# A fused attention and two-MLP kernel: the choice between two code paths moved to registers, the two paths' code swapped, the first loads made larger, and a new instruction order

## The chip, the cores and the metric

The kernel runs on one NeuronCore of a Trainium2 chip. The time is device microseconds of one launch: 628.85 us is the median of three runs (628.22 to 629.81). The engines are named as the profile names them: PE (TensorE, matmuls; PEld is its weight load), DVE (VectorE), ACT (ScalarE), POOL (GpSimd) and SP (SyncE, which here only issues transfers). Each has its own instruction stream and runs it in order; semaphores tie them together.

## The reference

The input is q, k, v for 2 batches, 8 heads, 768 positions and 64 dimensions, and three weight sets. Two scalars, `n_sink` = 4 and `window` = 128, say which keys a query sees.

```python
scores = scale * np.matmul(q, k.transpose(0, 1, 3, 2))
keep = is_sink | in_window               # key < n_sink, or 0 <= query - key < window
scores = np.where(keep, scores, -1000000000.0)
scores = scores - np.max(scores, axis=-1, keepdims=True)
a = np.exp(scores)
a = a / (np.sum(a, axis=-1, keepdims=True) + 1e-09)
attn = np.matmul(a, v)                   # heads joined: x is 1536 x 512
# first MLP
h = x @ w_in                             # 512 x 2048
g = np.where(h >= 1, h, np.where(h <= -1, 0.0, (h + 1) ** 2 / 4))
x = g @ w_out
# second MLP, d_ff = 1536
out = (1 / (1 + np.exp(-(x @ w_gate))) * (x @ w_val)) @ w_out2
```

## The kernel before, in words

The two scalars are inputs, so the program holds two paths. The banded path works where `n_sink` is at most 16 and `window` at most 129; it looks at 16 sink keys and two blocks of 128 keys per tile of 112 queries. The dense path takes any other values. The inputs of the runs take the banded path. Each engine's stream is: a common opening, a branch, the code of one path, the code of the other, and a common end.

The opening (`moe_chain_kernel`) loads the two scalars (`nw`), and q and k of the first two query tiles and v of the first, for the four head pairs, each pair in a transfer of its own, half of them issued by SP and half by ACT. POOL makes an identity matrix (`ident`), PE runs six matmuls on it, and POOL and DVE make the first mask. Then PE computes the scores of the first tile of all four pairs into two PSUM banks (L1242), DVE takes the row maxima of them (`row_tops`, L1186, eight times), and a flag, computed on POOL and DVE from the scalars and left in SBUF, is read by every engine into a register (L1246) and compared (L1247).

Before the diff the banded path's code stands right behind this branch, and the dense path's code behind it. So on the banded path the branch at L1247 goes straight on, and a jump at the end of the path leads over the dense path's code to the common end, where SP waits for the last transfers.

The banded path is not written in its final order. `Body.banded` and `Body.moe` record operations with reads, writes, a duration and a due time. `Plan.order` then places them by a list schedule: on each engine, the ready operation with the earliest due time comes first. A table of numbers at the top (`START`, `READY`, `FINISH`, `MOE_DUE`, `MOE_PACE`, `DRAIN`, `EARLY`, `LATE`, `SAME_MODE`, `BIAS`) sets when each engine is thought to begin and how early each kind is due. What comes out is fixed: nothing is chosen at run time. Where PE would stand idle in the plan's first 55 us, `Plan.fillers` puts matmuls of the identity on itself (L354), whose results nobody reads.

Per query tile and head pair PE does: scores (L927), transposes of the exponentials (L941), values (L968); per tile, four transposes that spread the inverse sums (L991). DVE takes row maxima (L1186) and the scaling (L982, L983, L1003), ACT the exponentials (L933) and most copies out of PSUM (L358). All of the second tile onwards is loaded by SP (L874).

Between these stand matmuls of the first MLP (L551 to L553, L596 to L598) on tokens that attention has finished. Its weights come as int64 words that hold float64 bits; SP loads them (`st`, L448), ACT or POOL rescales (L452, L454) and DVE does four more steps (L457, L460, L463, L466), then they are split in a high and a low part. After attention PE does the rest of the first MLP and the second one (L713, L799 to L801), and SP writes the result (L811) while the last matmuls run.

Of the kernel before, what the change touches and what calls it, by code (L numbers as in the profile page):

```python
# [51 lines left out]
DMA_LAT = 2.7  # L52
START = {"ACT": 0.9, "DVE": 2.1, "PE": 1.0, "SP": 1.1}
READY = {"tops": 0.2, "next": 0.5, "values": 1.5}

BIAS = {"DVE": 0.38, "POOL": 0.06, "ACT": -0.07}

SLOT_DUE = 2.55

FINISH = {"top": 3.59, "exp": 11.24, "turn": 13.87, "pts": 4.86, "values": -2.54, "div": 5.08, "out": -6.02}  # L60
MOE_DUE = 65.7
MOE_PACE = 5.86
DRAIN = 8.5
EARLY = 15.01
LATE = 62.91

ENTER, LEAVE = {"rows": 0.18, "cols": 0.14}, 0.09
SCORES_OF = 2
VALUES_OF = 4
SAME_MODE = 4.27  # L70
WARM = 6
# [70 lines left out]
class Plan:  # L142
# [40 lines left out]
    def order(self):  # L183
# [3 lines left out]
        free = {e: START.get(e, 0.0) for e in engines}  # L187
        held = {"DVE": 0.0, "POOL": 0.0}
        for o in self.ops:
            o.left = len(o.deps)  # L190
            for d in o.deps:
                d.next.append(o)
            if not o.left:
                for e in o.on:
                    ready[e].append((0.0, o))
        done, events, now, order, mode = 0, sorted({0.0, *START.values()}), 0.0, [], None
        running = []
# [105 lines left out]
class Body:  # L303
# [534 lines left out]


    def banded(self):  # L840

# [23 lines left out]
        def slot(k, due):  # L865
# [10 lines left out]
            mine, before = ("qk", p, at), ("qk", p, 1 - at)  # L876
            src = lambda j: self.a["qk"][b, j, p]
            if t < RAW:
                c0, first = pre["raw"][p]
                held = lambda j: cells("acc", 0, c0 + j * NQK, c0 + (j + 1) * NQK)  # L880
                own = lambda: pre["acc"][:, c0 + t * NQK:c0 + (t + 1) * NQK]
                rq = [k for j in (t - 1, t) if j >= 0 for k in held(j)]
            else:
                own, rq = (lambda: block(p, at)), [mine, before] if i else [mine]
            if t == 0:
                v, rv = (lambda: first), cells("acc", 0, c0 - P, c0)
                op("PRE", 0.0, 0.0, lambda: None, [], held(0), lat=0.0)
                op("PRE", 0.0, 0.0, lambda: None, [], held(1), lat=READY["next"] + 0.3 * p)
                op("PRE", 0.0, 0.0, lambda: None, [], rv, lat=READY["values"] + 0.2 * p)
# [14 lines left out]
            pt, pts = Buf(pt_r), Buf(pts_r)  # L904
            pr, mx = (Buf(pr_r), Buf(mx_r)) if t else (Kept(pre["rows"](p)), Kept(pre["mx"][:, 2 * p:2 * p + 2]))
            in_ring = [pr, mx] if t else []
            at_pr = [] if t else cells("acc", 0, pre["pr"][p], pre["pr"][p] + 2 * P)

            def keys(es):

                x = kept[p][es]
                if t < RAW:
                    a0 = c0 + (t - 1) * NQK + TQ
                    return pre["acc"][es, a0:a0 + 2 * (NQK + NS)].rearrange("p (c n) -> p c n", c=2)[:, :, :P]
# [119 lines left out]
    def dense(self):  # L1034

        nc, NP, S = self.nc, self.NP, self.S
        ident, lim = self.pre["ident"], limits(nc, self.pool(self.ctx, "lim"), self.pre["nf"])
        nk = S // P
# [56 lines left out]

FIRST_FLAG = 0x3F800000


def banded_test(nc, const, nf):

    ends, fits = const.tile([1, 8], F32, name="ends"), const.tile([1, 8], F32, name="fits")
    low, high, x = ends[:, :4], ends[:, 4:], nf[0:1].rearrange("p i w -> p (i w)")
    a, b = fits[:, :4], fits[:, 4:]
    v = nc.gpsimd
    for t, values in ((low, (0, 1)), (high, (NS, P + 1))):
        v.memset(t, 0.0)
        for i, y in enumerate(values):
            if y:
                v.memset(t[:, 2 * i:2 * i + 1], float(y))
    v.tensor_tensor(out=a, in0=x, in1=low, op=ALU.subtract)  # L1110
    v.tensor_tensor(out=b, in0=high, in1=x, op=ALU.subtract)
    return a, b


def banded_flag(nc, const, fits):


    a, b = fits
    flag = const.tile([1, 1], F32, name="flag")
    nc.vector.tensor_tensor_reduce(out=a, in0=a, in1=b, op0=ALU.mult, op1=ALU.max, scale=-1.0, scalar=0.25, accum_out=flag)  # L1120
    return flag.bitcast(I32)

# [67 lines left out]
def moe_chain_kernel(ctx: ExitStack, tc: tile.TileContext, a, out):  # L1190
# [9 lines left out]
        "acc": big.tile([P, KD * NT], F32, name="acc"),  # L1200
        "raw": [],
    }
    with tc.manual_schedule():

        nw, nf = const.tile([P, 4], I32, name="nw"), const.tile([P, 2, 2], F32, name="nf")
        nc.sync.dma_start(out=nw, in_=a["sizes"].bitcast(I32).rearrange("(o n) -> o n", o=1).to_broadcast([P, 4]))
        pre["nf"] = nf

        pairs = [(p, p * NT + S - TQ - 2 * NS, (nc.sync, nc.scalar)[p % 2]) for p in range(NP)]
        for p, c0, queue in pairs:  # L1210
            queue.dma_start(out=pre["acc"][:, c0:c0 + NQK], in_=a["qk"][0, 0, p])
        for p, c0, queue in pairs:
            queue.dma_start(out=pre["acc"][:, c0 + NQK:c0 + 2 * NQK], in_=a["qk"][0, 1, p])
        for p, c0, queue in pairs:
            v = pre["acc"][:, c0 - P:c0]
            queue.dma_start(out=v, in_=a["vb"][0, 0, p, :, 1])
            pre["raw"].append((c0, v.rearrange("p (c d) -> p c d", c=1)))
        nc.vector.tensor_copy(out=nf, in_=nw.rearrange("p (i w) -> p i w", i=2))
        pre["ident"] = const.tile([P, P], F32, name="ident")
# [7 lines left out]
        for i in range(WARM):  # L1227
            nc.tensor.matmul(out=pre["psum"][0][:, :P], lhsT=pre["ident"], rhs=pre["ident"], start=i == 0, stop=i == WARM - 1)
        pre["masks"] = masks = Masks(nc, const, nf, pre["acc"])
        fits = banded_test(nc, const, nf)  # L1230
        masks.make_first()
        flag = banded_flag(nc, const, fits)
        masks.weigh(masks.first)
        pre["mx"] = const.tile([TQ, 2 * NP], F32, name="mx0")
        pre["pr"] = [pairs[p // 2][1] + 3 * NQK + p % 2 * 2 * P for p in range(NP)]
        rows = lambda p: pre["acc"][:TQ, pre["pr"][p]:pre["pr"][p] + 2 * P].rearrange("p (e n) -> p e n", e=2)
        pre["rows"] = rows
        first = [pre["psum"][6 + e][:TQ].rearrange("p (i n) -> p i n", i=NP) for e in range(2)]
        for p, c0, _ in pairs:
            for e in range(2):  # L1240
                x = pre["acc"][64 * e:64 * e + 64, c0:c0 + NQK]
                nc.tensor.matmul(out=first[e][:, p], lhsT=x[:, :TQ], rhs=x[:, TQ + NS:], start=True, stop=True)  # L1242
        for p in range(NP):
            for e in range(2):
                row_tops(nc, rows(p)[:, e], first[e][:, p], masks.first, pre["mx"][:, 2 * p + e:2 * p + e + 1])
        on = nc.values_load(flag[0:1, 0:1], min_val=0, max_val=0x7F800000)  # L1246
    with tc.If(on < FIRST_FLAG) as branch:  # L1247
        with tc.manual_schedule(), ExitStack() as arm:
            body = Body(arm, tc, a, out, pre)
            body.banded()  # L1250
            body.moe(1)
            body.plan.run(body.banks, body.fill)
    with branch.Else():
        with tc.manual_schedule(), ExitStack() as arm:
            body = Body(arm, tc, a, out, pre)
            body.dense()
            body.moe(0)
            body.plan.run()


def layouts(inputs):
# [11 lines left out]
    vp = np.pad(vN, ((0, 0), (0, 0), (P, P), (0, 0)))  # L1273
    qk = np.zeros((B, len(tiles), NP, P, NQK), q.dtype)
    vb = np.zeros((B, len(tiles), NP, P, 2, P), v.dtype)
    for i, (q0, n) in enumerate(tiles):
        new = np.concatenate([kT[..., :NS], kp[..., P + q0 - NS:P + q0 + TQ]], axis=-1)
        qk[:, i, :, :, :n] = qT[:, :, :, q0:q0 + n]
        qk[:, i, :, :, TQ:] = new
        vv = np.concatenate([vN[:, :, :NS], vp[:, :, q0:q0 + W2 - NS]], axis=2)  # L1280
# [9 lines left out]
    def bands(w):  # L1290
# [5 lines left out]
        "v": np.ascontiguousarray(vN.reshape(B, NP, S // P, P, 2 * D).transpose(0, 1, 3, 2, 4)),  # L1296
        "qk": qk,
        "vb": vb,
        "w1": chunks(inputs["moe_w_in"]),
# [25 lines left out]
```

## Time and profile before

| | |
|---|---|
| runs, median | 628.85 us |
| profiled execution, its own time | 628.65 us |
| its span, first to last instruction | 626.9 us |
| around the span | 1.75 us |
| PE busy | 617.7 us, 3532 instructions |
| DVE busy | 509.4 us |
| ACT busy | 322.1 us |
| POOL busy | 90.3 us |
| HBM read, written | 50.60 MB, 3.15 MB |

The span is one execution on the chip. "Busy" of PE counts pipelined matmuls, so it says that matmuls followed each other, not how full the array was. A timeline row gives the start, the length of the merged stretch, the engine, the line of the kernel and the operation, the operands as output<-input, and in brackets how long the engine stood idle before it and what ended that. SPq and PEldq are the sequencers of SP and PE, which issue transfers, read registers and branch; that time is not counted as busy.

### The profile page before, as it was taken

What the parts mean: (1) busy time and instruction counts of PE and PEld (TensorE: products, weight loads), DVE (VectorE), ACT (ScalarE), POOL (GpSimd) and SP (SyncE); (2) the same over time, 40 slices, a digit from 0 to 9 for tenths busy, and PEclk for the clock granted to TensorE, in tenths of its full rate; (3) what the DMA queues carried; (4) which work ended last, traced back from release to release, by engine and by line L of the source; (5) the groups of instructions that cost most, each with busy time, mean ns of one, the idle gap of its engine ahead of it and who ended that gap; (6) DMA issues with size and microseconds to landing.
All of it is one profiled execution on the core that took longest, in us unless ns stands there. A gap on an engine that the chain in (4) does not pass through costs nothing.

```text
span 626.9 us, 9877 instructions
## 1 busy us (share of the span) xinstructions
PE 617.7 (99%) x3532; PEld 540.1 (86%) x3532; DVE 509.4 (81%) x1103; ACT 322.1 (51%) x738; POOL 90.3 (14%) x114
## 2 busy tenths in 40 slices
PE   8999999999999999999999999999999999999996
PEld 6788888888888888888888999998998998998995
DVE  5899998999996984458968797698898898895373
ACT  6999997656532441234335576563452452541430
POOL 1103320301000330012014320011011111120000
PEclk9999999999999999999999999999999999999999
DMA  6876764151540310001300012221221222100004
GB/s 200 261 214 195 231 183 158 62 198 38 167 135 4 114 55 30 1 0 35 101 35 0 1 35 98 72 101 33 81 89 54 81 68 78 58 0 1 1 36 172
DMA packets 28571, 54.48 MB, mean 87 GB/s; under 512 B 3296, under 2 KB 18400, under 8 KB 28512
## 3 DMA queue, kind: packets, MB, share of 16 engines
q1 hardware_dynamic: 27648, 53.10, 26.0%
q8 instruction: 30, 0.49, 0.3%
q10 hardware_dynamic: 864, 0.66, 0.3%
q14 instruction: 29, 0.24, 0.1%
HBM read 50.60 MB, written 3.15 MB: 86 GB/s over the span
## 4 chain that ended last, share of the span: by engine, by line
PE 95%; DMA 2%; SPq 2%; DVE 0%; ACT 0%; issue 0%; POOL 0%; POOLq 0%
PE bank L713 28%; PE bank L596 7%; PE bank L551 7%; PE bank L552 7%; PE bank L597 7%; PE bank L598 7%; PE bank L553 7%; PE bank L800 5%; PE bank L801 5%; PE bank L799 5%; PE bank L968 3%; PE bank L941 3%; PE bank L927 2%; SPq L874 1%; DMA st<-in_w 1%; PE bank L991 1%
## 5 line engine op out<-in xcount | busy, mean ns | idle before, releaser
L713 PE MATMUL bank<-xh,early 128*128 128x384 f32 x384 | 107.3, 334 | 0.0
L713 PE MATMUL bank<-late,early 128*128 128x384 f32 x432 | 85.0, 335 | 0.0
L713 PEld LDWEIGHTS bank<-late,early 128*128 128x128 f32 x432 | 76.0, 188 | 0.9
L358 ACT ACTIVATE early<-w 128x512 fp32r<-128x512 f32 (+1 forms) x59 | 35.4, 601 | 78.4 <-PE bank L713 34.6
L713 PEld LDWEIGHTS bank<-xh,early 128*128 128x128 f32 x384 | 70.2, 188 | 0.2
L713 PE MATMUL bank<-xl,early 128*128 128x384 f32 x192 | 64.2, 334 | 0.0
L809 DVE TENSOR_TENSOR acc<-bank,acc 128x512 f32<-128x512 f32 (+1 forms) x61 | 40.6, 677 | 23.8 <-PE bank L801 23.7
L570 ACT ACTIVATE tmp<-tmp 128x512 f32<-128x512 f32 x48 | 30.2, 631 | 46.5 <-DVE tmp L567 46.3
L933 ACT ACTIVATE pr<-pr,mx 112x256 f32<-112x256 f32 (+2 forms) x104 | 50.9, 494 | 0.1
L452 ACT ACTIVATE w<-st 128x512 f32<-128x512 f32 x60 | 39.4, 668 | 21.7 <-DMA st<-in_w 8.2
L463 DVE SCALAR_TENSOR_TENSOR w<-st,w 128x512 int32<-128x512 int32 x68 | 48.1, 708 | 0.7
L466 DVE SCALAR_TENSOR_TENSOR w<-st,w 128x512 int32<-128x512 int32 x68 | 46.9, 690 | 0.7
L365 DVE TENSOR_TENSOR early<-w,early 128x512 fp32r<-128x512 f32 (+1 forms) x63 | 40.4, 643 | 4.4 <-ACT early L358 4.4
L567 DVE TENSOR_SCALAR tmp<-bank 128x512 f32<-128x512 f32 x48 | 32.6, 683 | 14.0 <-PE bank L553 13.7
L358 ACT ACTIVATE gs<-tmp 128x512 fp32r<-128x512 f32 (+1 forms) x51 | 31.7, 623 | 23.3 <-DVE tmp L573 22.4
L612 DVE TENSOR_TENSOR acc<-bank,acc 128x512 f32<-128x512 f32 x36 | 24.3, 688 | 22.3 <-PE bank L598 22.2
L365 DVE TENSOR_TENSOR gs<-tmp,gs 128x512 fp32r<-128x512 f32 (+1 forms) x51 | 36.7, 723 | 6.4 <-ACT gs L358 5.8
L551 PE MATMUL bank<-xh,early 128*128 128x512 f32 x96 | 38.1, 397 | 0.0
L1186 DVE CUSTOM_DVE_ANT_0 pr<-bank,mask 112x256 f32<-112x256 f32 (+2 forms) x104 | 37.6, 403 | 0.5 <-PE bank L927 0.3
L596 PE MATMUL bank<-gs,early 128*128 128x512 f32 x96 | 37.9, 395 | 0.0
L552 PE MATMUL bank<-xl,early 128*128 128x512 f32 x96 | 37.5, 390 | 0.0
L553 PE MATMUL bank<-xh,early 128*128 128x512 f32 x96 | 37.5, 390 | 0.0
(179 smaller groups left out, 1490.2 us busy)
## 6 DMA issues: line engine op xcount, KB each, us to landing
st<-in_w SPq DMA_DIRECT2D x32, 512.0 KB, 3.5
v<-in_vb SPq DMA_DIRECT2D x52, 128.0 KB, 3.0
qk<-in_qk SPq DMA_DIRECT2D x48, 128.0 KB, 3.2
st<-in_wg SPq DMA_DIRECT2D x12, 512.0 KB, 3.3
st<-in_wv SPq DMA_DIRECT2D x12, 512.0 KB, 3.2
st<-in_wo SPq DMA_DIRECT2D x12, 512.0 KB, 3.3
out<-acc SPq DMA_DIRECT2D x11, 256.0 KB, 2.2
acc<-in_qk SPq DMA_DIRECT2D x8, 128.0 KB, 3.3
```

The costliest lines, as they stand in the source:

```text
L358: self.nc.scalar.activation(out=out, in_=x, func=AF.Copy)
L365: (self.nc.vector if e == "DVE" else self.nc.gpsimd).tensor_tensor(out=out, in0=x, in1=y, op=ALU.subtract)
L463: nc.vector.scalar_tensor_tensor(out=t(), in0=high(), scalar=-0x80000000, in1=t(), op0=ALU.bitwise_and, op1=ALU.bitwise_or)
L466: nc.vector.scalar_tensor_tensor(out=t(), in0=low(), scalar=29, in1=t(), op0=ALU.logical_shift_right, op1=ALU.bitwise_or)
L551: mm(out=out, lhsT=wh[:, c], rhs=mh, start=k == 0, stop=False)
L552: mm(out=out, lhsT=wh[:, c], rhs=ml, start=False, stop=False)
L553: mm(out=out, lhsT=wl[:, c], rhs=mh, start=False, stop=k == KD - 1)
L596: mm(out=out, lhsT=wh[:, c], rhs=gh, start=f == fs[0], stop=False)
L597: mm(out=out, lhsT=wh[:, c], rhs=gl, start=False, stop=False)
L598: mm(out=out, lhsT=wl[:, c], rhs=gh, start=False, stop=f == fs[-1])
L713: nc.tensor.matmul(out=out, lhsT=w[:, c], rhs=m, start=start and i == n == 0, stop=i == 1 and n == 2, skip_group_check=True)
L933: nc.scalar.activation(out=pr.ap[:n, e, :ks * P], in_=pr.ap[:n, e, :ks * P], func=AF.Exp, bias=mx.ap[:n, e:e + 1], scale=-1.0, accum_out=s ...
```

## The change

Five things change.

- The flag and its computation go (`banded_test`, `banded_flag`). `out_of_bands` lets each engine read the four words of the two scalars out of DRAM into registers right at the start, and compare them there.
- The branch now asks for the dense path. The dense path's code stands first and the banded path's code last, right ahead of the common end.
- The cast of the scalars, the first mask, the first tile's scores and their row maxima move behind the branch, into the banded path (`sizes`, `first_tops`). The scores of the four pairs and two heads go to eight PSUM banks instead of two.
- The first loads are five transfers instead of twelve: q and k of two head pairs together (256 KB, the layout of `qk` is changed for it), and v of all four pairs in one (`v0`).
- The table of numbers is another one, so the banded path's order is another one. The places where the first tiles lie in `acc` move with the loads.

```diff
-START = {"ACT": 0.9, "DVE": 2.1, "PE": 1.0, "SP": 1.1}
+START = {"ACT": 0.3, "DVE": 1.9, "SP": -1.5}
...
-EARLY = 15.01
-LATE = 62.91
+EARLY = 42.414
+LATE = -12.112
...
+    def first_tops(self):
+        nc, masks, NP = self.nc, self.pre["masks"], self.NP
+        self.sizes()
+        masks.make_first()
+        masks.weigh(masks.first)
+        for p in range(NP):
+            for e in range(2):
+                x = self.acc[64 * e:64 * e + 64, self.pre["raw"][0] + p * NQK:][:, :NQK]
+                nc.tensor.matmul(out=self.psum[2 * p + e][:TQ, :P], lhsT=x[:, :TQ], rhs=x[:, TQ + NS:], start=True, stop=True)
+        for p in range(NP):
+            for e in range(2):
+                row_tops(nc, self.rows(p)[:, e], self.psum[2 * p + e][:TQ, :P], masks.first, self.pre["mx"][:, 2 * p + e:2 * p + e + 1])
...
+def out_of_bands(nc, sizes):
+    words = sizes.bitcast(I32).rearrange("(o n) -> o n", o=1)
+    _, (ns, ns_high, win, win_high) = nc.values_load_multi_w_load_instructions(words, min_val=-2 ** 31, max_val=2 ** 31 - 1)
+    return (ns < 0) | (ns > NS) | (ns_high < 0) | (ns_high > 0) | (win < 1) | (win > P + 1) | (win_high < 0) | (win_high > 0)
...
+        raw, first_v = pre["raw"], pre["acc"][:, 3 * NT + TOK:3 * NT + 2 * TOK]
+        for t in range(2):
+            for h, queue in enumerate((nc.sync, nc.scalar)):
+                c = raw[t] + h * 2 * NQK
+                queue.dma_start(out=pre["acc"][:, c:c + 2 * NQK], in_=a["qk"][0, t, h].rearrange("p i n -> p (i n)"))
+        nc.scalar.dma_start(out=first_v, in_=a["v0"])
+        far = out_of_bands(nc, a["sizes"])
...
-        on = nc.values_load(flag[0:1, 0:1], min_val=0, max_val=0x7F800000)
-    with tc.If(on < FIRST_FLAG) as branch:
-            body.banded()
-            body.moe(1)
-            body.plan.run(body.banks, body.fill)
-    with branch.Else():
+    with tc.If(far > 0) as branch:
             body.dense()
             body.moe(0)
             body.plan.run()
+    with branch.Else():
+            body.first_tops()
+            body.banded()
+            body.moe(1)
+            body.plan.run(body.banks, body.fill)
```

On PE the start of the stream shows the moved branch. Before, the first tile's scores (L1242) and the read of the flag stand ahead of it:

```order
L1321 UNCONDITIONAL_BRANCH
L1228 MATMUL bank_92<-ident 128x128 x6
L1242 MATMUL bank_98<-acc 112x128
L1242 MATMUL bank_99<-acc 112x128
...
L1246 TENSOR_LOAD flag
L1247 COMPARE_AND_BRANCH
L927 MATMUL bank_92<-acc 112x256
```

Now two register reads (a pointer, then the four words) stand ahead of the six identity matmuls, and fifteen register operations ahead of the branch:

```order
L1311 UNCONDITIONAL_BRANCH
L1124 TENSOR_LOAD in_sizes_ptr
L1124 TENSOR_LOAD in_sizes
L1231 MATMUL bank_132<-ident 128x128 x6
L1234 REGISTER_ALU x15
L1234 COMPARE_AND_BRANCH
```

The dense path's rows follow; its last is the jump below, and the banded path starts behind it, some 3000 rows further on:

```order
L1234 UNCONDITIONAL_BRANCH
L858 MATMUL bank_125<-acc 112x128
L858 MATMUL bank_126<-acc 112x128
...
L858 MATMUL bank_132<-acc 112x128
L951 MATMUL bank_125<-acc 112x256
L951 MATMUL bank_126<-acc 112x256
```

So the first scores (now L858, banks 125 to 132) and the second tile's (now L951) both stand behind a branch that is taken.

On DVE the place is the first step on a weight (`w`), the clamp that follows POOL's rescaling. Before, it stands behind twenty row maxima of 256 columns; these are the last rows ahead of it and the first behind it:

```order
L1186 ISA pr,mx<-bank_96,mask_114 112x256
L1186 ISA mx 112x1
L1186 ISA pr,mx<-bank_93,mask_114 112x256
L1186 ISA mx 112x1
L457 TENSOR_SCALAR w<-w 128x512
L1003 TENSOR_TENSOR on<-on,bank_98 128x448
L982 TENSOR_SCALAR sm<-sm 112x8
L983 RECIPROCAL sm<-sm 112x8
```

Now it stands behind twenty-two of them, and a finished tile's two halves (`xh`, `xl`) stand ahead of it as before:

```order
L362 CAST xh<-on 128x4x112
L1190 ISA pr,mx<-bank_130,mask_147 112x256
L1190 ISA mx 112x1
L367 TENSOR_TENSOR xl<-on,xh 128x4x112
L1190 ISA pr,mx<-bank_128,mask_147 112x256
L1190 ISA mx 112x1
L1190 ISA pr,mx<-bank_125,mask_147 112x256
L1190 ISA mx 112x1
L459 TENSOR_SCALAR w<-w 128x512
L1190 ISA pr,mx<-bank_128,mask_147 112x256
```

The clamp moved two row maxima later. Over the whole banded path PE's operations are the same in kind and number, but for the identity matmuls between them, of which there are nine before (L354) and seven now (L356). Ahead of the first matmul of the MLP stand 52 scores and 72 values before, and 64 and 88 now.

## Rows read from the trace of the kernel before

**Rows 1.** Busy time by stretch: start:end, length, then each engine; granted clock.

```profile
0.00:5.00 5.00, 2.93 (x12) 2.64 (x12) 0.53 (x4) 0.00 (x0) 2.30 (x16) 1.00 0.44 132
6.60:45.00 38.40, 36.70 (x384) 29.38 (x385) 35.03 (x164) 37.17 (x135) 3.29 (x5) 1.00 0.79 243
45.00:621.70 576.70, 576.68 (x3121) 507.14 (x3120) 472.77 (x934) 284.00 (x605) 84.70 (x93) 1.00 0.23 75
```

**Rows 2.** What PE waited for: us in total, times, longest.

```profile
PE bank L927 <- DMA qk<-in_qk: 0.5, 1, 0.5
PE bank L991 <- DVE ie L360: 0.5, 1, 0.5
PE bank L941 <- ACT acc L933: 0.4, 1, 0.4
PE bank L991 <- ACT pr L933: 0.2, 1, 0.2
```

**Rows 3.** Timeline of the opening: start us, us, engine, line, operation, idle before.

```profile
0.73 0.20 POOL masks.py:197 MEMSET ident<- 128x128 f32 x1 [0.29 <-POOLq L1315]
1.35 2.93 PE L1228 MATMUL bank<-ident 128*128 128x128 f32 x12 [1.35 <-POOL ident masks.py:199]
5.02 1.44 PE L1242 MATMUL bank<-acc 64*112 64x128 f32 x16 [0.73 <-DMA acc<-in_qk]
6.62 1.99 PE L927 MATMUL bank<-acc 64*112 64x256 f32 x16 [0.17 <-DMA acc<-in_qk]
7.27 1.76 SPq L874 DMA_DIRECT2D v<-in_vb  x4
10.84 1.16 PE L354 MATMUL bank<-ident 128*128 128x128 f32 x8
```

**Rows 4.** Register reads and register operations of the flag: engine, operation, ns min/median/max, start.

```profile
L1246 PEldq TENSOR_LOAD <-flag x1: 485/485/485, 5.8 to 5.8; - x1
L1246 SPq FUSED_REGOPS  x1: 186/186/186, 6.9 to 6.9; - x1
L1246 DVEq TENSOR_LOAD <-flag x1: 542/542/542, 7.0 to 7.0; - x1
L1246 SPq SEQ_ASSERT  x1: 28/28/28, 7.1 to 7.1; - x1
```

**Rows 5.** The opening's read of the two scalars as a transfer: KB, us to landing.

```profile
nw<-in_sizes SPq DMA_DIRECT2D x1, 2.0 KB, 3.5
```

**Rows 6.** Branch and jump by engine: ns min/median/max, first to last start.

```profile
L1247 PEldq COMPARE_BRANCH  x2: 92/1878/3665, 6.4 to 618.8; - x2
L1247 SPq COMPARE_BRANCH  x2: 46/48/49, 7.2 to 622.6; - x2
```

**Rows 7.** SP's first instructions behind the jump: same columns.

```profile
L1321 SPq EVENT_SEMAPHORE  x10: 17/28/28, 625.5 to 626.8; - x10
```

**Rows 8.** The last seven output transfers, from 615 us on: issue, then landing in us.

```profile
L811 SPq DMA_DIRECT2D out<-acc x7: 332/333/446, 615.6 to 622.2; - x7
...
DMA to landing us min/median/max: 2.0/2.3/3.6
```

**Rows 9.** Code fetches ("instruction") in the transfers from 622.6 to 625.9 us.

```profile
q14 instruction: 3, 0.02, 2.7%
q8 instruction: 1, 0.02, 2.7%
```

**Rows 10.** Timeline around the first weight: POOL, DVE, PE.

```profile
22.54 0.67 POOL L454 TENSOR_SCALAR w<-st 128x512 f32<-128x512 f32 x1 [17.68 <-DMA st<-in_w]
23.25 0.43 DVE L457 TENSOR_SCALAR w<-w 128x512 f32<-128x512 f32 x1 [2.27 <-POOL w L454]
24.08 1.12 PE L927 MATMUL bank<-qk 64*112 64x256 f32 x8 [0.53 <-DMA qk<-in_qk]
32.01 0.57 PE L991 MATMUL bank<-ident,ie 112*128 112x112 f32 x4 [0.23 <-ACT pr L933]
```

**Rows 11.** A row maximum before 21 us: ns min/median/max, first to last start.

```profile
L1186 DVE CUSTOM_DVE_ANT_0 pr<-bank,mask x20: 371/420/425, 9.7 to 20.6; 112x256 f32<-112x256 f32 x20
```

More of the change, by code (lines that the diff above doesn't have):

```diff
@@ L52 @@
 DMA_LAT = 2.7
-START = {"ACT": 0.9, "DVE": 2.1, "PE": 1.0, "SP": 1.1}
[L54 to L63, printed above, removed]
-EARLY = 15.01
-LATE = 62.91
+START = {"ACT": 0.3, "DVE": 1.9, "SP": -1.5}
+READY = {"tops": 0.35, "next": (0.3, 0.5), "values": 1.0}
+BIAS = {"DVE": 0.693, "POOL": 0.41, "ACT": 0.365}
+SLOT_DUE = 2.235
+FINISH = {"top": -1.623, "exp": 2.295, "turn": 17.535, "pts": -3.643, "values": -3.859, "div": -7.538, "out": -23.001}
+MOE_DUE = 66.798
+MOE_PACE = 7.359
+DRAIN = 16.75
+EARLY = 42.414
+LATE = -12.112
 ENTER, LEAVE = {"rows": 0.18, "cols": 0.14}, 0.09
@@ L69 @@
 VALUES_OF = 4
-SAME_MODE = 4.27
+SAME_MODE = 6.12
 WARM = 6
@@ L188, in order @@
         held = {"DVE": 0.0, "POOL": 0.0}
+        events = sorted({0.0, *START.values()})
+        early = events[0]
         for o in self.ops:
@@ L194, in order @@
                 for e in o.on:
-                    ready[e].append((0.0, o))
-        done, events, now, order, mode = 0, sorted({0.0, *START.values()}), 0.0, [], None
+                    ready[e].append((early, o))
+        done, now, order, mode = 0, early, [], None
         running = []
@@ L837, in moe, with sizes, rows @@
             self.gated(p)
+    def sizes(self):
+        self.nc.vector.tensor_copy(out=self.pre["nf"], in_=self.pre["nw"].rearrange("p (i w) -> p i w", i=2))
+    def rows(self, p):
+        c = self.pre["pr"][p]
+        return self.acc[:TQ, c:c + W2].rearrange("p (e n) -> p e n", e=2)
+    def first_tops(self):
[10 more added lines that the diff above has]
+                row_tops(nc, self.rows(p)[:, e], self.psum[2 * p + e][:TQ, :P], masks.first, self.pre["mx"][:, 2 * p + e:2 * p + e + 1])
     def banded(self):
@@ L1200, in moe_chain_kernel @@
         "acc": big.tile([P, KD * NT], F32, name="acc"),
-        "raw": [],
+        "raw": [t * NT + TOK for t in range(RAW)],
+        "pr": [c + i * W2 for c in (3 * NT + 2 * TOK, NT) for i in range(2)],
     }
@@ L1227, in moe_chain_kernel @@
         for i in range(WARM):
[L1228 to L1233, printed above, removed]
-        pre["mx"] = const.tile([TQ, 2 * NP], F32, name="mx0")
[L1235 to L1245, printed above, removed]
-        on = nc.values_load(flag[0:1, 0:1], min_val=0, max_val=0x7F800000)
-    with tc.If(on < FIRST_FLAG) as branch:
-        with tc.manual_schedule(), ExitStack() as arm:
-            body = Body(arm, tc, a, out, pre)
-            body.banded()
-            body.moe(1)
-            body.plan.run(body.banks, body.fill)
-    with branch.Else():
+            nc.tensor.matmul(out=pre["psum"][7][:, :P], lhsT=pre["ident"], rhs=pre["ident"], start=i == 0, stop=i == WARM - 1)
+        pre["masks"] = Masks(nc, const, nf, pre["acc"])
+        pre["mx"] = const.tile([TQ, 2 * NP], F32, name="mx0")
+    with tc.If(far > 0) as branch:
         with tc.manual_schedule(), ExitStack() as arm:
@@ L1258, in moe_chain_kernel @@
             body.plan.run()
+    with branch.Else():
+        with tc.manual_schedule(), ExitStack() as arm:
+            body = Body(arm, tc, a, out, pre)
+            body.first_tops()
+            body.banded()
+            body.moe(1)
+            body.plan.run(body.banks, body.fill)
 def layouts(inputs):
```

62 lines of the change are left out of this document (19 added, 43 removed).

## The prediction, on record before the changed kernel ran

> **What bounds the kernel now.** I read the busy time by stretch first [rows 1]. [...] In the first 5 us there are only the identity matmuls. [...] The work itself is the same; the order lists the same PE operations but for two identity matmuls. The waits of PE come next: four behind the branch, 1.6 us together [rows 2], and 0.17 at 6.62 [rows 3]; the last of them ends at 32.0 [rows 10]. Then the opening in order of time [rows 3], the branch and the end.
>
> The profiled execution took 628.65 us, its span and 1.75 us around it; the median of the runs is 628.85. I sum against 628.65 and compare with 628.85; differences under 0.3% (1.9 us) count as no change, being about what a measurement of this kernel can tell.
>
> **The opening.** Before, PE starts on the second tile's scores at 6.62 us [rows 3]; all that follows on PE hangs on that start. Now each engine must read registers, compare, take a branch and get code that does not lie next to it. The steps on PE:
>
> - Entry at 0.73 us, when POOL began before [rows 3].
> - Two register reads. Read out of SBUF one word took 0.49 us on PE and 0.54 on DVE [rows 4]. The trace has no read out of DRAM. Its bounds are that 0.5 from below and, far off, a whole transfer of the same words, 3.5 us [rows 5], from above, so 1.0 to 7.0 for the two. I take 1.0, since the row is the same instruction. POOL makes its two reads ahead of `ident`, so PE's identity matmuls begin 0.62 us (1.35 - 0.73) after 1.73, at 2.35, instead of 1.35.
> - Fifteen register operations. Rows near it are an assertion of 28 ns and a fused pair of 186 ns [rows 4], so 0.03 to 0.09 each, 0.4 to 1.4 together; I take 0.9: 3.25 us.
> - The branch and the code. Before, it goes straight on and costs 92 ns on PE at 6.4 us. The jump at the end of the path shows what going elsewhere costs: 3.67 us on PE, 2.9 on SP (622.6 to 625.5) [rows 6, 7]. 3.25 + 3.7 is 6.95 us. PE's eight first scores take 0.9 (sixteen passes of L1242; their 1.44 us holds a wait for the second loads).
>
> The second tile's scores then begin at 7.85 instead of 6.62: **+1.2 us**. The lower bound is where the loads bind again: the first q and k landed at 5.0, so 5.9, a gain of 0.7. With reads of 3.5 us each the upper bound is 13.9, a loss of 7.2. DVE goes the same way and has cast and mask to make while PE does the first scores; I cost that at nothing too, or up to 1 us if DVE comes no earlier than PE. SP issues three loads first and pays 2.9, so it enters within 0.5 us of its 7.27 before [rows 3]. The five larger loads hide behind the branch, as do the eight banks; I cost both at nothing. If the branch were free, the data would bind, and larger loads would then be worth the 0.17 that PE waited at 6.6 [rows 3].
>
> [...]
>
> **What PE loses up to 45 us.** DVE stood 2.27 us before its clamp of the first weight at 23.25, since POOL waited for its load until 22.54 [rows 10]. PE's waits of 0.5, 0.5 and 0.2 us lie behind it, at 24 to 32 us [rows 10], one of them on DVE's `ie` [rows 2]. In the new order the clamp stands two row maxima later, 0.42 us each [rows 11], and DVE itself is about 1.2 late while SP's load is 0.5 late. The stall shrinks to 2.3 - 0.8 - 1.2 + 0.5, about 0.8. PE has twelve more scores and sixteen more values ahead of its first MLP matmul, so it can bridge that. I count the three waits as gone, **-1.2 us**, bounds 0 (they come back elsewhere) and -1.8 (all of them). The wait for the first exponentials, 0.4, stays. Two identity matmuls fewer: eight passes took 1.16 us [rows 3], so a matmul of two passes is 0.23 to 0.29, and two are **-0.45**, provided their gaps are really closed; else 0. From 45 us on I cost the new order at nothing. PE has covered all of it there, and if a weight came late, each us of delay would show in full.
>
> **The end.** The last issue is at 622.2 us, and its landing took 3.6, to 625.8; the median of the seven last is 2.3, the lowest 2.0 [rows 8]. The same stretch has four fetches of code [rows 9], those of the jump, on the same transfer engines. SP itself is back only at 625.5 [rows 7]. Without the jump both go: 622.2 + 2.3 is 624.5, **-1.3 us**, bounds 0 (the late packet had another cause; SP's return then hides in it) and -1.6.
>
> **Sum.** 628.65 + 1.2 - 1.2 - 0.45 - 1.3 = 626.9 us, 1.95 under the median, just past the bound of 1.9.
>
> **The rivals.**
>
> - *A deeper gain.* The code comes while PE would wait for data anyway. Then the scores begin at 5.9 and the opening gives -0.7: 628.65 - 0.7 - 1.2 - 0.45 - 1.3 = 625.0. For it speaks that everything up to 5.0 us is idle for PE [rows 1]; against it, that the fetch cannot begin before the registers are known, and 3.67 us from 3.25 ends behind 5.0. Chance 0.22.
> - *The two ends cancel.* The reads out of DRAM are slower: the geometric mean of 0.49 and 3.5 [rows 4, 5], 1.3 us each, makes the opening +2.8 and the sum 628.5. That such a read goes further than one out of SBUF speaks for it. Chance 0.20. [...]
> - *Slower: PE enters late and at half rate.* PE's twelve passes on `ident` took 2.93 us, 0.23 each, where later ones took 0.12 to 0.14 [rows 3], while the granted clock reads 1.00 [rows 1]. Before, 0.73 us of rest stood between them and the scores. Now they end near 5.3 and PE rests until it has its code. If fetches of five engines in turn hold it until 9.5 (2.5 later than summed) and it has fallen back by then, first and second scores take 0.9 + 1.7 us more: 626.9 + 2.5 + 2.6 = 632.0. It decides from the point where opening and half rate together cost 4.85, past the 2.95 that the other terms give and the 1.9 of the bound. Against it: with a rest of 2 us or less nothing in this trace shows a fall. Chance 0.14. [...]
>
> That the change does not do what it says could be true of the banks alone: if DVE's mask comes later than the first scores, eight banks change nothing. The sum holds that already.
>
> **How the numbers follow.** The forecast, 626.9 with its own range 625.7 to 628.0, gets 0.44; the rivals 0.22, 0.20 and 0.14. Faster by over 0.3% (under 626.97) is half of the forecast's, 0.23, and the deeper gain, 0.22, and a little of the second: 0.47. Slower by over 0.3% is nearly all of the last, 0.13. Same is the rest, 0.40. The range leaves out about a tenth on each side: 624.4 to 629.8.
>
> **What would show it.** Right: DVE's and PE's branch near 3 us and the next instruction some 3 us later; the second tile's scores between 7.3 and 8.5 us; no PE wait over 0.3 us between 20 and 45 us; the last output transfer landing within 2.4 us, with SP already waiting for it. Wrong: scores before 6.6 us (the fetch hides), register reads over 1 us each, identity-like pitch of 0.23 us in the first scores, a wait of PE after 45 us, or a last landing as late as before.

## The result, and the profile after

The changed kernel takes 636.35 us, the median of 6 runs (634.83 to 636.52); beside it the kernel before took 629.44 (628.22 to 630.03). The ratio is 1.0106, with a 95% interval of 1.0091 to 1.0121. The forecast was 626.9, within 624.4 to 629.8: the change went the other way. The profiled execution took 636.37 us, with a span of 634.6.

The first view is the busy time by stretch of the kernel after (start:end, length, then PE, PEld, DVE, ACT, POOL, the granted clock, DMA share and GB/s). They answer to the stretches of [rows 1]: from the second tile's scores to 45 us, from there to the last matmul, and the end.

```profile
12.30:45.00 32.70, 30.33 (x310) 23.50 (x307) 29.21 (x132) 29.00 (x106) 3.14 (x4) 1.00 0.76 231
45.00:631.40 586.40, 584.18 (x3197) 512.53 (x3194) 485.19 (x941) 285.30 (x614) 121.36 (x124) 1.00 0.24 77
631.40:634.60 3.20, 0.03 (x1) 0.00 (x0) 0.42 (x1) 0.00 (x0) 0.00 (x0) 1.00 0.45 164
```

Against the spans of before these rows give the whole difference of 7.7 us:

| | before | after | difference |
|---|---|---|---|
| second tile's scores begin at | 6.6 | 12.3 | +5.7 |
| PE idle from there to 45 us | 38.40 - 36.70 = 1.70 | 32.70 - 30.33 = 2.37 | +0.7 |
| PE idle from 45 us to the last matmul | 0.02 | 586.40 - 584.18 = 2.22 | +2.2 |
| PE busy in both stretches | 613.38 | 614.51 | +1.1 |
| from the last matmul to the end | 626.9 - 621.7 = 5.2 | 3.2 | -2.0 |

PE's busy time is longer though it has two identity matmuls fewer: the thirty-two passes of scores on `acc` took 5.1 us, 4.2 before. The opening lost most. Here is its timeline, in the columns of [rows 3]:

```profile
4.71 0.20 POOL masks.py:197 MEMSET ident<- 128x128 f32 x1 [4.26 <-issue]
5.33 2.93 PE L1231 MATMUL bank<-ident 128*128 128x128 f32 x12 [5.33 <-POOL ident masks.py:199]
9.24 0.17 DVE L843 CAST nf<-nw 128x4 f32<-128x4 int32 x1 [9.24 <-issue]
10.51 2.05 PE L858 MATMUL bank<-acc 64*112 64x128 f32 x16 [2.24 <-issue]
10.95 2.94 SPq L897 DMA_DIRECT2D v<-in_vb  x4
12.32 1.09 PE L951 MATMUL bank<-acc 64*112 64x256 f32 x4
13.97 1.55 PE L951 MATMUL bank<-acc 64*112 64x256 f32 x12 [0.55 <-issue]
```

PE's scores of the second tile stand at 12.32 where they stood at 6.62, and after four passes they stop until 13.97: "issue" says that PE waits for nothing that the profile shows. That it waits for its next instructions is a reading: among the transfers a packet of code ("q8 instruction"), taken here for PE's, stands between 10.9 and 12.6 us, as another does at 7.9 behind the branch. SP enters the path at 10.95 instead of 7.27.

The register reads of the same stretch (engine, operation, ns min/median/max, start):

```profile
L1124 PEldq TENSOR_LOAD <-in_sizes_ptr x1: 946/946/946, 0.8 to 0.8; - x1
L1124 PEldq TENSOR_LOAD <-in_sizes x1: 2878/2878/2878, 1.8 to 1.8; - x1
L1124 SPq TENSOR_LOAD <-in_sizes_ptr x1: 2778/2778/2778, 2.1 to 2.1; - x1
L1124 SPq TENSOR_LOAD <-in_sizes x1: 888/888/888, 4.9 to 4.9; - x1
```

The reader is to see that it is not the kind of read that makes it slow: PE's first and SP's second take 0.9 us, and all that are under way between 2.2 and 4.6 us, the five engines' together, take 2.8 to 3.0. Then the register operations and the branch, in the same columns:

```profile
L1234 PEldq ALU_OP  x15: 37/43/43, 5.4 to 6.8; - x15
L1234 PEldq COMPARE_BRANCH  x1: 3349/3349/3349, 6.9 to 6.9; - x1
```

Fifteen operations take 1.5 us, 0.1 each from start to start, and the branch 3.35. What PE waits for behind 12.3 us (us in total, times, longest) answers to [rows 2]:

```profile
PE bank L951 <- DMA acc<-in_qk: 1.0, 1, 1.0
PE bank L951 <- DMA qk<-in_qk: 0.8, 2, 0.5
PE bank L715 <- DVE bank L362: 0.7, 1, 0.7
PE bank L951 <- issue: 0.6, 1, 0.6
PE bank L1015 <- POOL xh L364: 0.5, 1, 0.5
PE bank L1015 <- DVE mx L1190: 0.5, 1, 0.5
PE bank L965 <- DVE on L1027: 0.4, 1, 0.4
```

And the last outputs, against the 2.0/2.3/3.6 of [rows 8]:

```profile
DMA to landing us min/median/max: 1.7/2.0/2.0
```

### The profile page after: what moved, and what is told of

It reads as the page before. It is cut to its first block, busy times and chain, and to the rows that moved or that the text cites. A ratio compares the mean times of both kernels' runs of the same rounds, so it can differ in the third digit from the quotient of the medians.

```text
span 634.6 us, 9924 instructions
## 1 busy us (share of the span) xinstructions
PE 619.3 (98%) x3528; PEld 540.5 (85%) x3528; DVE 516.9 (81%) x1086; ACT 316.4 (50%) x723; POOL 126.2 (20%) x137
## 4 chain that ended last, share of the span: by engine, by line
PE 91%; DVE 5%; SPq 2%; DMA 1%; issue 1%; POOL 0%; ACT 0%; DVEq 0%
PE bank L715 27%; PE bank L598 7%; PE bank L599 7%; PE bank L600 7%; PE bank L553 6%; PE bank L554 6%; PE bank L555 6%; PE bank L803 5%; PE bank L802 5%; PE bank L801 5%; PE bank L951 3%; PE bank L992 3%; PE bank L965 3%; DMA qk<-in_qk 1%; PE bank L1015 1%
## 5 line engine op out<-in xcount | busy, mean ns | idle before, releaser
L360 ACT ACTIVATE early<-w 128x512 fp32r<-128x512 f32 (+1 forms) x46 | 26.3, 573 | 74.7 <-PE bank L803 28.1
L468 DVE SCALAR_TENSOR_TENSOR w<-st,w 128x512 int32<-128x512 int32 x68 | 51.7, 761 | 0.7
L465 DVE SCALAR_TENSOR_TENSOR w<-st,w 128x512 int32<-128x512 int32 x68 | 47.5, 698 | 0.6
L454 ACT ACTIVATE w<-st 128x512 f32<-128x512 f32 x61 | 40.3, 666 | 12.7 <-DMA st<-in_w 6.9
L367 DVE TENSOR_TENSOR early<-w,early 128x512 fp32r<-128x512 f32 (+1 forms) x53 | 37.1, 702 | 5.8 <-POOL early L364 5.4
L367 DVE TENSOR_TENSOR gs<-tmp,gs 128x512 fp32r<-128x512 f32 (+1 forms) x49 | 35.2, 719 | 4.6 <-ACT gs L360 4.0
L364 POOL TENSOR_SCALAR early<-w 128x512 fp32r<-128x512 f32 x19 | 13.7, 719 | 123.6 <-PE bank L715 58.2
```

Of the source, the lines that this page charges most:

```text
L360: self.nc.scalar.activation(out=out, in_=x, func=AF.Copy)
L367: (self.nc.vector if e == "DVE" else self.nc.gpsimd).tensor_tensor(out=out, in0=x, in1=y, op=ALU.subtract)
L465: nc.vector.scalar_tensor_tensor(out=t(), in0=high(), scalar=-0x80000000, in1=t(), op0=ALU.bitwise_and, op1=ALU.bitwise_or)
L468: nc.vector.scalar_tensor_tensor(out=t(), in0=low(), scalar=29, in1=t(), op0=ALU.logical_shift_right, op1=ALU.bitwise_or)
```

## The experiments

Fifteen kernels were run, each beside the kernel before on the same chip; ratios are to that. Four of them and the changed kernel form a ladder, in which each step adds one part of the change:

| step | median | ratio to before, 95% interval |
|---|---|---|
| large first loads | 629.78 | 1.0016 (1.0007 to 1.0024) |
| and register reads | 630.92 | 1.0020 (1.0012 to 1.0029) |
| and first scores behind the branch, eight banks | 630.32 | 1.0017 (1.0006 to 1.0028) |
| and the dense path's code first | 634.30 | 1.0082 (1.0065 to 1.0100) |
| and the new table: the changed kernel | 636.35 | 1.0106 (1.0091 to 1.0121) |

So two of the five parts carry the loss, 4.0 and 2.1 us; the other three cost 1 us together. By the ratios they are 4.1 and 1.5 us, and the intervals of the last two rows overlap, so the table's share is the less certain one.

### The code swap

The changed kernel with the banded path first again:

```diff
-    with tc.If(far > 0) as branch:      # dense, Else: banded
+    with tc.If(far < 1) as branch:      # banded, Else: dense
```

> The changed kernel with the banded path's code ahead of the dense path's again; all else as changed. Theory (code that a taken branch goes to must be fetched, 3.35 us on PE at 6.9 us, and once more between 12.8 and 14.0): PE's branch under 0.3 us, first scores near 7.9 instead of 10.5, no gap of over 0.5 us in the second tile's scores, SP in the path near 8.1 instead of 10.95; PE gains 3.7 to 5 us, the jump at the end costs 2 again: 633 to 635 us. Rival (the register reads out of DRAM are the cost, and the code would have to be fetched on a straight path too): the opening stays, the end adds 2: about 638 us.

Measured: 633.57 us, 1.0065 (1.0052 to 1.0078), 2.8 below the changed kernel. PE's branch there:

```profile
L1234 PEldq COMPARE_BRANCH  x2: 95/1898/3702, 6.8 to 624.2; - x2
```

95 ns at 6.8 us, and 3.7 us for the jump at 624.2. SP enters at 8.00, and the first scores and the second tile's follow each other without a gap:

```profile
8.08 2.05 PE L858 MATMUL bank<-acc 64*112 64x128 f32 x16
9.92 2.33 PE L951 MATMUL bank<-acc 64*112 64x256 f32 x16
```

The theory holds. The first scores are at half pitch here too (sixteen passes in 2.05 us, 1.13 in the next run), with no rest ahead of them.

Next, with the dense path's code left out altogether:

```diff
     with tc.If(far > 0) as branch:
-            body.dense() ...
+            pass
```

> The changed kernel with the dense path's code left out (the other arm is empty), so the taken branch goes a few instructions ahead. Theory (distance is what costs: the code behind is then at hand): PE's branch under 0.5 us, first scores near 7.9, PE gains 3.7 to 5 us, the end as in the changed kernel: 631 to 633 us. Rival (any taken branch throws away what was fetched ahead): branch 2 to 3.4 us as now, 636 us.

Measured: 631.60 us, 1.0034 (1.0021 to 1.0047). This is a taken branch too, but a short one:

```profile
L1234 PEldq COMPARE_BRANCH  x1: 232/232/232, 6.9 to 6.9; - x1
8.17 1.13 PE L858 MATMUL bank<-acc 64*112 64x128 f32 x16
```

What costs is the distance, not that the branch is taken: 0.23 us here, 3.35 over the dense path's code. This kernel has neither the late entry nor the jump at the end. The swap alone on the kernel before (`on < FIRST_FLAG` turned to `on >= FIRST_FLAG`, the two bodies exchanged):

> The kernel before with one edit: the dense path's code ahead of the banded path's. Flag in SBUF, scores ahead of the branch, loads and order as before. Theory (a taken branch to far code costs PE 3.35 us, and a second stall of 1 us follows): PE's branch near 6.4 us takes 3.3 to 3.7, second tile's scores at 9.9 instead of 6.62, SP in the path near 10.2 instead of 7.27; the end 2 us shorter: 631.5 to 633 us. Rival (the fetch lies beside row maxima and exponentials that are to be done anyway): scores before 8.5, 627.5 to 629 us.

Measured: 632.27 us, 1.0052 (1.0036 to 1.0067). PE's branch takes 3.75 us at 6.4, the second tile's scores begin at 10.30, 3.7 later, and run at half the pitch:

```profile
5.03 2.05 PE L1242 MATMUL bank<-acc 64*112 64x128 f32 x16 [0.76 <-DMA acc<-in_qk]
10.30 4.18 PE L927 MATMUL bank<-acc 64*112 64x256 f32 x16 [3.22 <-issue]
```

Sixteen passes of L927 took 1.99 us before [rows 3] and 4.18 here. So this kernel loses the rest itself and goes on at half pitch. That the second follows from the first is not shown: PE was at half pitch ahead of the branch already (the 2.05 us), and two kernels without a far branch, with the large loads alone and with the new table alone, took 3.62 and 3.55 us for the same sixteen passes (below). The last matmul ends 5.9 us later (627.6 for 621.7), which is 3.7 + 2.2, and the end is 1.9 shorter. The second stall that the theory named did not come.

### The register reads and the fetch

`out_of_bands` moved ahead of the loads on SP and ACT:

```diff
+        far = out_of_bands(nc, a["sizes"])
         nc.sync.dma_start(out=nw, ...)
         ...
-        far = out_of_bands(nc, a["sizes"])
```

> The changed kernel with the register reads ahead of the first loads on SP and ACT. Theory (the second read took 2.9 us since the first loads run at the same time; SP's and ACT's second reads, after them, took 0.9): every read 0.9 us, PE's and DVE's branch about 2 us earlier (near 4.9), loads issued 1.9 us later; the first scores then wait for the loads: 634.5 to 636.5 us. Rival (something other than the loads holds the reads until 4.6 us): reads still end near 4.6, loads land 3 to 4 us later: 637 to 640 us.

Measured: 635.18 us, 1.0094 (1.0080 to 1.0109). The reads took 0.96 and 0.53 us on PE:

```profile
L1124 PEldq TENSOR_LOAD <-in_sizes_ptr x1: 957/957/957, 0.8 to 0.8; - x1
L1124 PEldq TENSOR_LOAD <-in_sizes x1: 525/525/525, 1.8 to 1.8; - x1
```

The loads had slowed them, then: the same four words took 0.53 us here and 2.88 in the changed kernel. But the branch, now at 4.5 us, took the time back, and the first scores waited 5.1 us for no load, as the theory had it, but at "issue". Its two rows, here and with three of the five loads moved behind the branch, which leaves two fifths of the bytes ahead of it:

```profile
L1234 PEldq COMPARE_BRANCH  x1: 6289/6289/6289, 4.5 to 4.5; - x1
```

```diff
-        for t in range(2): (loads of tile t)
-        nc.scalar.dma_start(out=first_v, in_=a["v0"])
+        load(0)
...
+            load(1)                                   # in the banded path
+            nc.scalar.dma_start(out=first_v, in_=a["v0"])
             body.first_tops()
```

> The changed kernel with the register reads ahead of the loads on SP and ACT, as in the run of that name, and the loads of the second tile and of v moved behind the branch, so that a third of the bytes is in flight when the code is fetched. Theory (PE's code took 6.29 us there, and 3.35 in the changed kernel, since its fetch waits behind the loads): PE's branch 3.4 to 4.5 us from 4.5, first scores by 9.5, 632.5 to 634.5 us. Rival (something other than the loads holds the fetch): branch over 6 us, 635 to 637 us, since the second tile's loads now come later too.

```profile
L1234 PEldq COMPARE_BRANCH  x1: 4309/4309/4309, 4.5 to 4.5; - x1
```

4.31 us instead of 6.29 at the same start: the fetch waits behind the loads, as the theory has it. The transfers say the same: the packet taken for PE's code begins 3.9 us after the branch with all loads ahead of it (8.4 less 4.5), 1.9 with two of the five (6.4 less 4.5) and 1.0 in the changed kernel (7.9 less 6.9), where the loads are nearly done (DMA share 0.22 from 6.9 to 8.0 us, 0.74 here from 4.5 to 8.5). The time was missed: 636.67 us, 1.0119 (1.0097 to 1.0140), within the rival's range. The mask and the second tile came later, and PE, at half pitch (2.05 us for the first sixteen passes), waited 1.9 us for DVE. Reading earlier and loading less in front only move the wait.

### Large loads, and where the scores stand

The kernel before with the new loads and places alone, old flag, old table:

> The kernel before with the changed kernel's five large first loads and places in acc; flag, two banks, code order and table as before. Theory A (loads of the second tile bound PE by 0.17 us only): 628.8 to 629.6 us. Theory B (a transfer of 256 KB is usable only when whole, so the first scores begin 0.5 us later): first scores at 5.5 instead of 5.0, 629.8 us.

Measured: 629.78 us (12 runs), 1.0016. The time is theory B's, and the first scores come later than it said:

```profile
5.99 2.05 PE L1263 MATMUL bank<-acc 64*112 64x128 f32 x16 [1.71 <-DMA acc<-in_qk]
7.83 3.62 PE L951 MATMUL bank<-acc 64*112 64x256 f32 x16
```

They begin at 5.99 instead of 5.02 [rows 3]. The row shows that they wait for the transfer; that one pair's q and k are usable only when the transfer of two pairs is whole is the theory's reason, not tried by itself. Then the register reads on top (as in the diff of the change, scores still ahead of the branch, banded path first), and the scores behind the branch:

> As the run before, with the first scores and row maxima ahead of the branch in two banks, as in the kernel before; so against that kernel only large loads and register reads differ. Theory (POOL's reads of 3.8 us hold up the identity matrix, and PE's identity matmuls stand ahead of the first scores): first scores near 8.1 instead of 6.0 with large loads alone: 630.5 to 631.5 us. Rival (the reads lie beside the loads): 629.8 us, as large loads alone.

> The changed kernel with the table of before and the banded path's code first: what is left of the change is registers, large loads, and first scores behind the branch in eight banks. Theory (costs add: without the swap 0.7 to 3 less than the 634.3 of the changed kernel with the old table): 631 to 632.5 us, no wait of PE over 0.6 us behind the branch. Rival (the late opening alone is the loss, wherever the code lies): 634 us.

Measured: 630.92 us, 1.0020 (1.0012 to 1.0029), first scores at 8.14; and 630.32 us, 1.0017 (1.0006 to 1.0028), first scores at 8.12 and the second tile's at 9.24. The first is as its theory said, the second 0.7 us under its theory's range. It has a row of waits that teaches much, all of PE's waits in the whole kernel:

```profile
PE bank L1231 <- POOL ident masks.py:199: 5.3, 1, 5.3
```

It stands ahead of these scores:

```profile
9.24 2.09 PE L951 MATMUL bank<-acc 64*112 64x256 f32 x16
```

Entering 2.6 us later (9.24 for 6.62), PE waits for nothing any more, and its last matmul ends at 622.7, only 1.1 later. The 1.7 us that PE waited in 6.6 to 45 us before are given back by being late.

### The order

The changed kernel with the old table:

> The changed kernel with the table of numbers of before (the order's planner), all else as changed. Theory A (PE's 2.2 us of waits behind 45 us come from the new order): they go, 634 us. Theory B (they come from loads that SP issues 3.7 us late): waits of the same sum elsewhere, 636 to 637 us.

Measured: 634.30 us (632.86 to 636.44), 1.0082 (1.0065 to 1.0100). Theory A has it right. In its profile PE waits 0.9 us behind the first scores, where the changed kernel waits 4.5 together:

```profile
PE bank L965 <- DVE tmp L575: 0.6, 1, 0.6
PE bank L599 <- DVE gs L367: 0.3, 1, 0.3
```

Among the 4.5 are 1.8 us for q and k. Here SP enters as late as there (10.81), and PE waits for no load, so the late entry does not make that wait by itself; the order has a part in it. The new table alone on the kernel before:

> The kernel before with only the table of numbers of the changed kernel (and the planner's early start that it needs). Theory A (the new order costs PE by itself; with the old one in the changed kernel the median was 2.05 lower): 631 to 632.5 us, with PE's waits of 0.4 to 0.9 us on DVE near 45 us and near 345. Theory B (the new order only suffers from the late opening): 629.3 within 1 us.

Measured: 632.73 us (632.44 to 634.31), 1.0066 (1.0052 to 1.0080); theory A again, and larger than said. Its waits on DVE and POOL are those of the changed kernel. The second tile's scores, and three of its stretches:

```profile
6.99 3.55 PE L929 MATMUL bank<-acc 64*112 64x256 f32 x16
45.00:330.00 285.00, 284.36 (x1589) 235.05 (x1590) 241.18 (x503) 148.34 (x329) 51.67 (x53) 1.00 0.30 96
330.00:380.00 50.00, 48.93 (x245) 43.79 (x245) 42.80 (x70) 28.29 (x59) 19.37 (x19) 1.00 0.04 11
380.00:620.00 240.00, 240.00 (x1263) 224.51 (x1262) 192.03 (x342) 101.90 (x203) 49.22 (x52) 1.00 0.18 60
```

Where before had PE busy without a break from 45 us on [rows 1], it stands 0.64 us up to 330 and 1.07 between 330 and 380. That is 1.7 of the 3.6 us by which its last matmul ends later (625.3 for 621.7). The other 1.9 are there at 10.5 us already, when the second tile's scores end: PE is at half pitch in this profile's opening (3.55 us for the sixteen passes, 1.99 before). Whether that is the table's doing is not shown, since kernels with the same opening differ in it (last section). Ahead of the wait behind 330:

```profile
338.01 1.25 POOL L367 TENSOR_TENSOR late<-acc,late 128x384 fp32r<-128x384 f32 x1 [0.17 <-ACT late L360]
338.31 1.36 DVE L367 TENSOR_TENSOR xl<-acc,xh 128x384 fp32r<-128x384 f32 x1
342.32 0.55 DVE L362 COPY bank<-bank 128x384 f32<-128x384 f32 x1
342.93 0.45 PE L715 MATMUL bank<-xh,early 128*128 128x384 f32 x1 [0.73 <-DVE bank L362]
```

DVE took 1.36 us for `xl` beside an operation of POOL; the same step took 0.54 in the kernel before, at 336.30, with POOL idle. The new table gives POOL more work (126.7 us busy, 90.3 before). DVE is then late with the copy that PE needs. That POOL's share is the cause of this wait was read from the trace, not tried by itself, and it cannot be all of it: with the MLP's numbers alone, the first of the three runs below, the same step takes 1.36 us at 338.92, beside an operation of POOL as well, and PE does not wait. Which entries cost the time was asked in three runs, each putting one group on the kernel before:

> The kernel before with only the new MOE_DUE, MOE_PACE, DRAIN, EARLY and LATE (first MLP's due times, its copies and loads). Theory A (copies out of PSUM are due 16.75 us ahead of their matmuls instead of 8.5 and weights are loaded earlier, so DVE serves them at the wrong time): PE's waits on DVE near 342 and 366, 1.4 us, are here: 630.4 to 631.5 us. Theory B (those entries only move work that is covered): within 0.7 us of before, 629.4.

> The kernel before with only the new BIAS and SLOT_DUE (which engine takes a copy, and attention's pace, 2.235 instead of 2.55 us per tile and pair). Theory A (attention is planned faster than DVE and ACT can go, so the MLP's matmuls, which could fill PE, come later than 44 us, and PE waits for DVE at 45 to 65): first MLP matmul after 48 us, 1 to 2 us of waits there, 630.4 to 631.5 us. Theory B (waits come from the MLP's entries): within 0.7 us of before, 629.4.

> The kernel before with only the new FINISH and SAME_MODE (due times within attention, and how long PE stays with one shape). Theory (neither waits near 345 nor a later MLP come from these): within 0.7 us of before, 629.4. Rival (values and divisions that are due up to 17 us later leave DVE's work until PE needs it): 630.4 us or more, PE waiting on DVE for a finished tile between 45 and 65 us.

Measured: 631.93 us, 1.0047 (1.0034 to 1.0061); 631.60, 1.0043 (1.0029 to 1.0057); 635.27, 1.0093 (1.0078 to 1.0109). Every group costs by itself, the last more than the whole table, and the waits that theory A put into the first two are in neither. Nor is the loss made of waits alone. With the second group PE waits no longer than before, but is busy 621.1 us for 617.7, and 2.3 of these 3.4 are identity matmuls, which the planner puts where PE would stand idle. The kernel before has eighteen passes of them, this one thirty:

```profile
L354 PE MATMUL bank<-ident 128*128 128x128 f32 x18 | 3.1, 288 | 0.0
L354 PE MATMUL bank<-ident 128*128 128x128 f32 x30 | 5.4, 299 | 0.2 <-DVE mx L1186 0.2
```

So what a group costs does not add up to what the table costs, and which of its numbers costs the 2 to 4 us stays open. The last run shows one more thing, PE's granted clock at 0.50 for 3.3 us, behind two waits of 1.3 and 0.7 us on ACT:

```profile
93.90:97.20 3.30, 3.30 (x30) 3.02 (x32) 2.59 (x16) 2.32 (x9) 0.62 (x1) 0.50 0.11 32
```

### PE's clock

The changed kernel with more identity matmuls:

```diff
-WARM = 6
+WARM = 14
```

> The changed kernel with 14 identity matmuls on PE instead of 6. Theory (PE's passes ran at twice the pitch until 13.4 us, since it rested from 8.3 to 10.5): the identity matmuls end near 10, the first scores take 1.1 us instead of 2.05, and the first second-tile scores 0.6 less: 634.8 to 635.5 us. Rival (identity matmuls ahead of the branch hold up the branch, and the fetch with it): branch later than 6.9, 636.4 to 637.5 us.

Measured: 640.54 us, 1.0179 (1.0165 to 1.0194), beyond even the rival. Its timeline of PE, and the granted clock by stretch:

```profile
5.36 5.24 PE L1231 MATMUL bank<-ident 128*128 128x128 f32 x28 [5.36 <-POOL ident masks.py:199]
13.19 0.95 PE L858 MATMUL bank<-acc 64*112 64x128 f32 x5 [2.59 <-issue]
16.75 1.41 PE L858 MATMUL bank<-acc 64*112 64x128 f32 x10 [2.61 <-issue]
```

```profile
9.30:12.60 3.30, 1.30 (x12) 1.10 (x10) 0.81 (x3) 0.00 (x0) 0.00 (x0) 1.00 0.23 55
12.70:22.90 10.20, 7.10 (x38) 6.13 (x39) 4.21 (x28) 3.43 (x16) 0.00 (x0) 0.50 0.75 219
```

The eight matmuls delay the register operations behind them (7.7 to 9.1 us, 5.4 to 6.8 in the changed kernel), and with them the branch, to 9.2 us (3.79 long). PE does reach full pitch at 9.3 (twelve passes in 1.30 us), rests from 10.6 to 13.2 at "issue", falls to a granted clock of 0.50 at 12.7 and stays there to 22.9. Here warming did not bridge the rest, since it pushed the rest along. On the kernel before, where the branch takes 92 ns [rows 6], `WARM` was raised to 9:

> The kernel before with 9 identity matmuls ahead of the first scores instead of 6, so that PE does not rest from 4.3 to 5.0 us. Theory (that rest decides whether PE reaches the higher clock level by 4.2 us, as in its profile, or only after 10, as in two kernels with the same opening): full pitch by 7.6 us, 627.4 to 628.4 us and a smaller spread than the 627.6 to 630.5 of before. Rival (the time at which the level rises has nothing to do with the rest): 628.9 us, same spread; or first scores 0.2 to 0.4 us later and that much slower.

Measured: 628.73 us (627.91 to 631.20, 12 runs), 0.9993 (0.9981 to 1.0006): no difference that can be told, and no smaller spread. In its profile the second tile's scores take 1.98 us, so PE was at full pitch by 6.6; but so it was in the profile of before (1.99), so the run does not say what an earlier rise is worth. This was the one version that might have beaten both kernels.

## Why the prediction was wrong, point by point

**The bound.** It was read from [rows 1]: three engines nearly level up to 45 us, then PE alone. That was right. It was the reason why 2.6 us of late entry cost only 1.1 in the ladder's third step.

**The opening, +1.2, measured +5.7.** Step by step: the two reads were taken at 1.0 from a read of SBUF and took 3.8 (bounds 1.0 to 7.0); the row for it was wrong in kind, because these reads met the loads, and the trace of before has no read out of DRAM at all. POOL's reads held `ident` to 5.3 and so PE's operations to 5.4; they took 1.5, not 0.9. The branch took 3.35, not 3.7: right. The first scores took 1.8 to the next, not 0.9, at half pitch. So 2.8 of the 4.5 us between 7.85 and 12.32 are the reads, 0.9 the pitch and 0.6 the operations. 0.82 + 3.83 + 0.75 + 1.5 + 3.35 + 0.26 + 1.81 is 12.32. Missed altogether: the second stop at 12.8 to 14.0, and SP's late entry. I had it within 0.5 us of 7.27, and it came 3.7 later (10.95). PE waited 1.8 us for q and k behind it; with the old table and SP as late it did not.

The step that failed is the overlap: "The five larger loads hide behind the branch", costed at nothing. Reads, fetch and loads were summed as if they did not meet, and they hold each other up. PE's two reads took 3.8 us beside the loads and 1.5 ahead of them; but then the branch began among the loads and took 6.29, and by medians the kernel gained only 1.2 us. So the price of the jump, taken from the end of the kernel, would hardly have held for a branch at 3.25 us either.

**Waits up to 45 us, -1.2, and two identity matmuls, -0.45; measured +0.7.** The waits on DVE's `ie` and on ACT are gone, as counted, but the one for q and k grew from 0.5 to 1.8 and the second stop came on top. The old waits vanish when PE is late, as the third step and the old table in the changed kernel show, so that gain is lateness, and no merit of the new order. I read more attention ahead of the first MLP matmul as a bridge; with the new table on the kernel before PE waited 0.4 and 0.5 us for DVE in attention, up to 44.0 and 45.1 us, ahead of that matmul at 50.1. The two identity matmuls fewer brought 0.1 us, not 0.45 (3.0 us in fourteen passes for 3.1 in eighteen).

**"From 45 us on I cost the new order at nothing": measured +2.2.** This is the second step that failed, a term put at nothing. I reasoned that PE had covered everything before, which says nothing of another order. By medians the table costs 3.9 us on the kernel before, 3.3 with the banded path first (633.57 less 630.32) and 2.1 in the changed kernel.

**The end, -1.3, measured -2.0.** Right in kind: the last landing fell from 3.6 to 1.7, and no jump follows it. The bound of -1.6 was too near, since it took the lowest landing of before, 2.0, and the last one now took 1.7.

**The rivals.** The slower one, PE entering late and at half rate, is what happened (first scores at 10.5, sixteen passes in 2.05 us instead of the 1.13 of the short branch). It had a chance of 0.14, a time of 632.0, and a fetch held up as its reason. PE entered late because of the second rival's reason, slow reads, with the fetch behind them. That it had fallen back by resting is not shown: it was not yet at full pitch before it rested, and with the banded path first the same passes took 2.05 us without a rest. None of the rivals held a dearer order, which is 2.1 of the 6.5 us by which the range ended short. The opening is most of the rest: 12.32 lies within its bounds (up to 13.9), but the range gave the upper part of them no room.

**Signs named beforehand.** "Register reads over 1 us each", the double pitch, and a wait of PE after 45 us were named as what would show the forecast wrong. The last two came, and the first for one of each engine's two reads.

## What to carry to other kernels

A jump over much code cost PE 3.35 to 3.8 us at the end of these kernels and at the start, and up to 6.3 among loads. At the end it cost 2 us of the time, since part of it lies beside other work; at the start nothing covered it. So the path that is taken should stand right behind the branch. A schedule that was tuned as a whole is priced by its waits and its filling matmuls in a run, not by what its list seems to bridge. And where engines are level, ask of each late start how much of it later waits give back: here 1.5 of 2.6 us.

## What was not expected of the hardware

- On PE the register read of the four words out of DRAM took 0.53 us and that of their pointer 0.96 ahead of the loads; while 1.25 MB of loads ran, the reads under way on the five engines took 2.8 to 3.0.
- A code fetch waits behind loads too, by these times: PE's branch took 3.35 and 3.75 us late in the loads, 4.31 with two of the five under way, 6.29 at the start of all of them. After a far branch a second stop can follow (1.2 us from start to start in the changed kernel, 2.6 idle with 14 identity matmuls); the swap alone on the kernel before has none.
- With the same opening, PE was at full pitch at 5.0 us in the profile of before (sixteen passes in 1.44 with a wait among them) and at half pitch there with the new table (2.05). The profile shows one execution, and the opening's pitch is not the same in each. The view's granted clock reads 1.00 in these stretches, and only the pitch tells, for the trace's first clock record, the one at 1.00, begins later: at 4.2 us before, at 10.4 with the new table on that kernel, and at 13.4 in the changed kernel.
